# Attention and FFN on one core: five batches' attention packed into FFN tiles 2 to 4, their inputs loaded as fp32, seven-product up-projection in tiles 5 to 8

## The chip, the core and the metric

One core of a Trainium2 chip runs the whole kernel. The metric is the device time of one execution in microseconds (us). The engines are named as in the profile: PE (matrix products; PEld is its weight load), DVE, ACT, POOL, and SP, which here only issues transfers.

## What is computed

```python
# q, k, v: (batch 8, heads 8, sequence 576, head dimension 64), fp32
scores = q @ k.T / sqrt(64)            # masked: a block of 64 rows sees its own and earlier blocks of 64
attn   = softmax(scores) @ v
x      = attn as (8 * 576, 512)
gate   = maximum(x @ w_gate, 0)        # w_gate, w_val: (512, 1536)
out    = (gate * (x @ w_val)) @ w_out  # w_out: (1536, 512), out fp32
```

## The kernel before

**Two halves that share the engines.** The FFN works on 9 tiles of 512 tokens. Tile j below 8 holds the first 512 tokens of batch j; tile 8 holds the last 64 tokens of all eight batches. The attention of a batch is four rounds (one for each pair of heads; round r belongs to batch r // 4). The attention of batch b has to be done before FFN tile b begins.

**A tile of the FFN** (`ffn_gen`). Plain: for each of 12 blocks of hidden units, 4 products for the gate and 4 for the value (L1095, 512 columns each), a relu on ACT (L1105) and a product of both on DVE (L1115). From tile `SEVEN = 2` on, the down-projection (`seven_products`, products in L793) uses a scheme of seven half-size block products in the place of eight, 84 products of 256 columns; it needs sums of hidden values, which DVE makes (L750, 14 calls a tile), copies of PSUM on ACT (L825) and adds on DVE (L829). From tile `UPS = 7` on, the up-projection (`seven_up`, L965) does the same: six units of 28 products of 256 columns. It needs sums of weights, made once on POOL (`up_sums`, L900), copies on ACT, adds on DVE (L992), and products on DVE and POOL (L997, L1001).

**A round of attention.** `visit` (L454) makes the scores of two heads and three groups of exponentials on ACT (L459, L466); `corners` sets the masked blocks to zero on DVE (L1263) or POOL (L1266); `head_av` multiplies by the values (L589, L603) and normalises (DVE, L526 to L535); the result `xnat` is transposed into `xT`, for batches 2 to 7 by a DMA transpose from SP (L638). From batch `FIRST = 3` on, the 64 tail tokens are done inside the rounds; their result goes by `xtail` into `xTt` (L575). `last_keys` (L476) makes the scores of the tail with itself.

**How q, k and v arrive.** Batches 0 to 2 (class `Early`): SP loads fp32 into `stage` tiles (10 of them, which the FFN's sums use too), a compute engine casts to bf16, and then either PE transposes, or (batch 2) SP issues a DMA transpose of 1024 columns into `perm` (L245) and a compute engine reorders `perm` into `qTm` or `kTm` (`unpermute`, L256). Batches 3 to 7 (`load_qkv`, L341): POOL issues loads that cast on their way, 17 to a batch, and SP issues two DMA transposes of 2048 columns (`dma_transposes`, L350) straight into `qTm` and `kTm`, and two for the tails (L119, L120).

**What sets the order.** The order is written out by hand: every piece of work has a name and a place in a table `AT`, and the places count steps of the FFN (one step is one product of 512 columns or two of 256; a tile is 144 or 138 steps). A loop takes the pieces in order of their places, and lets the FFN run up to the place before each. So on each engine the order is fixed, and an engine that waits holds up all that stands behind it in its own queue; between the engines only semaphores count. Names: `s`, `e`, `c`, `a`, `b`, `x` with a round's number are its scores, its last exponential, its corners, the two heads' products with the values, and its transpose into `xT`; `L3` is `last_keys(3)`. In the steady part a round came every 28 steps, and the attention of batch b + 1 lay in tile b:

```python
STEADY = {"s": 2, "e": 8, "c": 15, "a": 22, "b": 26, "x": 26.1}
...
for b in range(4, B):
    base = 144 * (b - 1)
    for i in range(4):
        ...
            AT[f"{n}{r}"] = base + 28 * i + p + (5 if i == 3 and n in "abx" else 0)
```

**PSUM.** Eight banks: four for scores (`sc`, two tiles of two banks), one named `one`, and three that the FFN and attention share (`ffnp`). When the last scores are done, the four of `sc` become the up-projection's banks (`upa`, `upc`).

## Time and profile before

| What | us |
|---|---|
| three runs: median (lowest to highest) | 358.78 (355.13 to 361.32) |
| the profiled execution: its time | 356.78 |
| its span, first to last instruction | 355.0 |
| busy: PE | 340.3 |
| busy: DVE | 214.9 |
| busy: ACT | 196.8 |
| busy: POOL (its loads among it) | 166.2 |

| Part of the span (chain of waits) | from, us | to, us |
|---|---|---|
| tile 2 (batch 3's attention and batch 2's tail in it) | 104.5 | 145.4 |
| tile 3 (batch 4's attention in it) | 145.4 | 182.8 |
| tile 7 (no attention) | 296.1 | 324.2 |

The profiled execution's time is that of the run; the span is what the trace covers, and 1.78 us lie around it. Busy times of engines overlap. Matrix products are pipelined: the mean of one (379 ns for 512 columns) is longer than the distance between two.

### The profile page before, as it was taken

What the parts mean: (1) busy time and instruction counts of PE and PEld (TensorE: products, weight loads), DVE (VectorE), ACT (ScalarE), POOL (GpSimd) and SP (SyncE); (2) the same over time, 40 slices, a digit from 0 to 9 for tenths busy, and PEclk for the clock granted to TensorE, in tenths of its full rate; (3) what the DMA queues carried; (4) which work ended last, traced back from release to release, by engine and by line L of the source; (5) the groups of instructions that cost most, each with busy time, mean ns of one, the idle gap of its engine ahead of it and who ended that gap; (6) DMA issues with size and microseconds to landing.
All of it is one profiled execution on the core that took longest, in us unless ns stands there. A gap on an engine that the chain in (4) does not pass through costs nothing.

```text
span 355.0 us, 8402 instructions
## 1 busy us (share of the span) xinstructions
PE 340.3 (96%) x3277; PEld 216.7 (61%) x3317; DVE 214.9 (61%) x552; ACT 196.8 (55%) x319; POOL 166.2 (47%) x199
## 2 busy tenths in 40 slices
PE   7899999999989999999999999999999999999994
PEld 3544455545434458555765577556855598888883
DVE  4664445668526766367626663567447757787783
ACT  4932756687235573655556554665276626735731
POOL 4647546589905900292009407970291042620630
PEclk9999999999999999999999999999999999999999
DMA  8999989999997997499539973999521013003005
GB/s 245 295 354 373 329 218 274 205 144 160 196 196 82 143 124 157 119 139 130 114 115 137 132 147 111 107 130 154 113 66 24 18 24 118 2 3 118 2 3 118
DMA packets 155496, 50.04 MB, mean 141 GB/s; under 512 B 134464, under 2 KB 151872, under 8 KB 155456
## 3 DMA queue, kind: packets, MB, share of 16 engines
q0 software_dynamic: 70480, 8.85, 47.4%
q1 hardware_dynamic: 79040, 33.96, 46.9%
q10 hardware_dynamic: 5936, 6.69, 5.9%
q8 instruction: 26, 0.43, 0.5%
q14 instruction: 14, 0.11, 0.1%
HBM read 37.75 MB, written 9.44 MB: 133 GB/s over the span
## 4 chain that ended last, share of the span: by engine, by line
PE 84%; ACT 5%; DMA 4%; DVE 3%; issue 2%; POOL 0%; DVEq 0%; POOLq 0%
PE ffnp L1095 37%; PE ffnp L793 12%; PE upa L965 6%; PE one L793 5%; PE ffnp L1199 3%; PE sc L454 3%; PE upc L965 3%; DMA xT<-xnat 2%; PE ffnp L589 2%; PE one L454 2%; DMA stage<-in_moe_w_gate_dram 2%; ACT attnT L418 2%; PE one L589 1%; PE ffnp L965 1%; ACT attnT L459 1%
## 5 line engine op out<-in xcount | busy, mean ns | idle before, releaser
L1115 DVE TENSOR_TENSOR hT<-gate_sb,ffnp 128x512 bf16<-128x512 bf16 x82 | 56.1, 684 | 63.9 <-PE ffnp L1095 33.1
L1095 PE MATMUL ffnp<-xT,wv 128*128 128x512 bf16 x309 | 87.3, 379 | 1.6 <-issue 0.6
L1095 PE MATMUL ffnp<-xT,wg 128*128 128x512 bf16 x301 | 84.9, 379 | 3.0 <-DMA xT<-xnat 1.7
L1105 ACT ACTIVATE gate_sb<-ffnp 128x512 bf16<-128x512 f32 x79 | 47.9, 609 | 49.2 <-PE ffnp L1095 49.2
L459 ACT ACTIVATE attnT<-sc 128x1024 bf16<-128x1024 f32 x56 | 57.6, 1043 | 0.0
L1095 PEld LDWEIGHTS <-wv 128*128 128x128 bf16 x336 | 30.3, 98 | 35.2 <-issue 5.2
L1095 PEld LDWEIGHTS <-wg 128*128 128x128 bf16 x336 | 30.6, 98 | 32.9 <-issue 3.6
L341 POOL DMA_DIRECT2D q_bf<-in_q_dram x20 | 17.9, 913 | 51.4 <-DVE hT L1115 37.2
L825 ACT COPY ob<-ffnp 128x512 f32<-128x512 f32 x21 | 12.3, 585 | 46.2 <-PE ffnp L793 44.7
L793 PEld LDWEIGHTS <-stage 128*128 128x128 bf16 x336 | 32.5, 98 | 3.6
L589 PEld LDWEIGHTS <-attnT 128*128 128x128 bf16 x640 | 26.5, 98 | 12.7 <-issue 1.9
L793 PEld LDWEIGHTS <-hT 128*128 128x128 bf16 x252 | 24.2, 98 | 4.5 <-DVE hT L997 0.7
L466 ACT ACTIVATE attnT<-one 128x512 bf16<-128x512 f32 (+1 forms) x28 | 15.0, 536 | 18.0 <-PE ffnp L454 17.8
L341 POOL DMA_DIRECT2D v_bf<-in_v_dram x30 | 24.2, 876 | 0.7 <-PE one L603 0.6
L1199 PE MATMUL ffnp<-wo,hT 128*128 128x512 bf16 x90 | 22.8, 379 | 0.3
L454 PEld LDWEIGHTS <-kTm 64*128 64x128 bf16 x384 | 13.3, 94 | 14.3 <-issue 8.3
L793 PE MATMUL ffnp<-stage 128*128 128x256 bf16 x168 | 21.4, 273 | 0.0
L793 PE MATMUL ffnp<-wo,hT 128*128 128x256 bf16 x168 | 21.3, 273 | 0.1
L750 DVE TENSOR_TENSOR stage<-hT 128x512 bf16<-128x512 bf16 (+1 forms) x45 | 17.6, 394 | 0.5
L454 PE MATMUL sc<-qTm,kTm 64*128 64x512 bf16 (+1 forms) x168 | 17.8, 305 | 0.0
L341 POOL DMA_DIRECT2D k_bf<-in_k_dram x20 | 17.7, 939 | 0.0
L1001 POOL TENSOR_TENSOR hT<-attnT,gate_sb 128x512 bf16<-128x512 f32 x4 | 4.6, 1162 | 25.1 <-ACT gate_sb L1009 25.1
(185 smaller groups left out, 617.8 us busy)
## 6 DMA issues: line engine op xcount, KB each, us to landing
out_dram<-ob ACTq DMA_DIRECT2D x24, 256.0 KB, 2.4
stage<-in_moe_w_val_dram SPq DMA_DIRECT2D x6, 512.0 KB, 8.3
stage<-in_moe_w_gate_dram SPq DMA_DIRECT2D x6, 512.0 KB, 8.7
stage<-in_moe_w_out_dram SPq DMA_DIRECT2D x6, 512.0 KB, 10.6
q_bf<-in_q_dram POOLq DMA_DIRECT2D x20, 128.0 KB, 4.7
k_bf<-in_k_dram POOLq DMA_DIRECT2D x20, 128.0 KB, 5.8
v_bf<-in_v_dram POOLq DMA_DIRECT2D x20, 128.0 KB, 6.3
stage<-in_v_dram SPq DMA_DIRECT2D x19, 128.0 KB, 5.6
```

The source lines that it names most:

```text
L341: ins = nc.gpsimd.dma_start(dst, part_of)
L454: nc.tensor.matmul(o, kTm[b % 2][head_of(hh), c, hp, :], qT, start=True, stop=True)
L459: return lambda: nc.scalar.activation(at[:, :, lo : lo + 512], sc, AF.Exp, scale=scale)
L466: nc.scalar.activation(at[:, hh, 1024 : 1024 + w], third[hh][:, 0:w], AF.Exp, scale=scale)
L589: nc.tensor.matmul(av[:, p, :], at[:, col : col + 128], v_bf[b % 2][:, c, h, :], start=(p == 0), stop=(c == p), skip_group_check=True,)
L750: ins = (eng or nc.vector).tensor_tensor(out=s(i), in0=a, in1=b, op=op)
L793: nc.tensor.matmul(to, sums.of(c)[which]()[:, 128 * p : 128 * p + 128], right, start=first, stop=(c == 5), skip_group_check=True,)
L965: nc.tensor.matmul(to[:, 256 * f : 256 * f + 256], left(which, u // 2)[:, kc, lo : lo + 128], right[which](kc), start=new and (f, kc) == ( ...
L1095: nc.tensor.matmul(to, (wg, wv)[t][f // 4][:, c, 128 * (f % 4) : 128 * (f % 4) + 128], x[:, c], start=(c == 0), stop=(c == 3),)
L1105: nc.scalar.activation(gate_sb, gate, AF.Relu)
L1115: nc.vector.tensor_tensor(out=h, in0=gate_sb, in1=val, op=AX.mult)
L1199: nc.tensor.matmul(op, hT[f][:, 128 * s : 128 * (s + 1)], wo[f // 4][:, f % 4, n0:n1], start=(f == 0), stop=(f == 11),)
```

## The change

Three things, which go together.

1. Batches 3 to 7 are loaded in the manner of batch 2: SP loads fp32 (q and k in halves of four heads, 512 KB each; v in two pairs of chunks; three tails), POOL, and for some pieces ACT, cast into `half` tiles (7 of them), SP issues four DMA transposes of 1024 columns into `perm`, and POOL reorders them (two copies for each pair of heads). POOL issues no loads any more. `load_qkv` and `dma_transposes` go.
2. Their rounds come every 18 steps from place 315 on, so that batches 3 to 7 are done in tiles 2 to 4. Their first head's product with v uses bank `one`, the second's a shared bank. All products go into `xT` by DMA transposes, as before; `xT` has four buffers in the place of three. Some corners (rounds 12, 13, 16, 21, 28, 29, 31) are zeroed by POOL.
3. `UPS` is 5: tiles 5 to 8 use the seven-product up-projection. Its weight sums move (places about 618 to 738, that is tile 4 and the first steps of tile 5), and those of its second and third part use other buffers. In tiles 2 to 4 the down-projection no longer uses bank `one`, which attention has; it does its products in another order with two banks, and product 5 goes into the bank of product 2. Stores of tiles 4 and 5 go from ACT's queue to SP's (that of the tiles from `UPS - 1` on).

Beside these, some 230 places are given one by one, for pieces of batches 0 to 2 too, most of them moved by a few steps.

```diff
-    UPS = 7
+    UPS = 5
+    HALVES = 7
...
-    def new_bf():
-        return [sb.tile([128, 2048], BF, name=n, bufs=2) for n in ("q_bf", "k_bf")]
+    def new_half():
+        return sb.tile([128, 1024], BF, name="half", bufs=HALVES)
...
-    def load_qkv(b, which, behind=None):
...
-    def dma_transposes(b, ts=(0, 1)):
...
-            xTs[b] = sb.tile([128, 4, 512], BF, name="xT", bufs=3)
+            xTs[b] = sb.tile([128, 4, 512], BF, name="xT", bufs=4)
...
+        if j < UPS:
+            yield from whole(a, 1, cs=range(5))
+            yield from whole(d, 2, cs=(0,))
+            yield from whole(a, 1, new=False, cs=(5,))
+            c11 = kept(a)
+            yield from whole(d, 2, new=False, cs=range(1, 6))
+            sums.step(13)
+            sums.step(14)
+            yield from whole(a, 6, new=False)
+            plus(d, c11)
+            c12 = kept(a)
+            c = d
+            yield from whole(c, 5)
...
         def late_up():
             last = units[5]
             yield from fourth(last)
-            sums.make(1, 1, 0, 2)
             hidden_0(last)
             mult(nc.vector, last, 1, last.s, last.g1)
-            for q, i in ((1, 2), (2, 1), (2, 2), (0, 3), (1, 3), (0, 4), (1, 4)):
+            for q, i in (
+                (1, 1), (1, 2), (2, 1), (2, 2), (0, 3), (1, 3), (0, 4), (1, 4)
+            ):
...
-        STEADY = {"s": 2, "e": 8, "c": 15, "a": 22, "b": 26, "x": 26.1}
+        STEADY = {"s": 0, "e": 6, "c": 12, "a": 24, "b": 28, "x": 28.1}
+        START, STEP = 315, 18
...
+            return {
+                f"Q{b}0": (-100, lambda: e.load_qk(0, 4)),
+                f"Q{b}4": (-92, lambda: e.load_qk(4, 4)),
+                f"V{b}0": (-72, lambda: e.load_v_chunks(0)),
+                f"V{b}1": (-64, lambda: e.load_v_chunks(1)),
+                f"T{b}": (-56, lambda: load_tails(e)),
+                f"K{b}0": (-88, lambda: e.cast_qk(0, 4, [by[n] for n in HOW[f"K{b}0"]])),
+                f"K{b}4": (-76, lambda: e.cast_qk(4, 4, [by[n] for n in HOW[f"K{b}4"]])),
+                f"P{b}0": (-87.9, lambda: e.transpose(0)),
+                f"P{b}4": (-71, lambda: e.transpose(1)),
+                **{
+                    f"u{b}{hp}": (p, unpermute(hp))
+                    for hp, p in enumerate((-62, -55, -42, -34))
+                },
+                f"w{b}0": (-50, lambda: e.cast_v_chunks(0, by[HOW[f"w{b}0"][0]])),
+                f"w{b}1": (-46, lambda: e.cast_v_chunks(1, by[HOW[f"w{b}1"][0]])),
+                f"tc{b}": (-38, lambda: e.cast_tails(True, 0, pool)),
+                f"td{b}": (-26, lambda: e.cast_tails(False, 1, dve)),
+                f"t{b}": (-25, e.transpose_tails),
+                f"L{b}": (9, lambda: last_keys(b)),
+            }
...
+                "K30": ("pool", "act"),
+                "K34": ("act", "pool"),
+                "K50": ("act", "pool"),
+                "K54": ("act", "pool"),
+                "c12": "pool",
+                "c13": "pool",
...
+            base = START + 4 * STEP * (b - FIRST)
...
-                AT[f"U{i}{s}"] = 144 * (4 + min(i, 1)) + 128 + 4 * i + s
-        AT["U23"], AT["U24"] = 144 * 6 + 115, 144 * 6 + 116
+                AT[f"U{i}{s}"] = place_at((288 + 330, 288 + 276 + 118, 288 + 414 + 18)[i]) + s / 8
...
+                "Q40": 295.64,
+                "Q44": 303.64,
+                "K40": 307.64,
+                "P40": 307.74,
...
+                "u40": 329.0,
+                "c12": 329.47,
```

Letters in the new table: `Q` loads q and k of four heads, `V` two chunks of v, `T` the tails; `K`, `w`, `tc`, `td` cast them; `P` transposes `half` into `perm`, `u` reorders `perm`, `t` transposes the tails. The first digit is the batch; the numbers are places in steps, those of the first list relative to the batch's first scores.

More of the change, by code (lines that the diff above doesn't have):

```diff
@@ L886, in up_sums @@
                 four = [sb.tile([128, 1024], BF, name="perm", bufs=4) for _ in range(4)]
-            else:
-                two = new_bf()
-                four = [t[:, 1024 * n : 1024 * n + 1024] for t in two for n in range(2)]
+            elif i == 1:
+                four = [new_half() for _ in range(4)]
+            else:
+                four = [
+                    t[0].rearrange("p c h n -> p (c h n)")[:, 1024 * n : 1024 * n + 1024]
+                    for t in (qTm, kTm)
+                    for n in range(2)
+                ]
             wsums.append([t.rearrange("p (c n) -> p c n", c=2) for t in four])
@@ L1735, with place_at, quarter, unpermute @@
             acts.update(tail_at(b))
-        for b in range(4, B):
-            base = 144 * (b - 1)
+        def place_at(p):
+            if p < 288:
+                return p
+            j, o = divmod(p - 288, 138)
+            return 144 * (j + 2) + min(o, 96) + max(0, o - 96) * 48 / 42
+        def quarter(b):
+            e = Early(b)
+            def unpermute(hp):
+                return lambda: e.unpermute(hp, [by[n] for n in HOW[f"u{b}{hp}"]])
+            return {
[19 more added lines that the diff above has]
+            }
@@ L1738 @@
+        for b in range(FIRST, B):
+            base = START + 4 * STEP * (b - FIRST)
             for i in range(4):
                 r = 4 * b + i
-                here = ("sc", "sc") if i == 3 else ("one", "ffn")
-                acts.update(round_at(r, ("dve", *here, None)))
+                acts.update(round_at(r, (HOW[f"c{r}"], "one", "ffn", None)))
                 for n, p in STEADY.items():
-                    AT[f"{n}{r}"] = base + 28 * i + p + (5 if i == 3 and n in "abx" else 0)
-            acts[f"L{b}"] = lambda b=b: last_keys(b)
```

422 lines of the change are left out of this document (294 added, 128 removed), and 3 rows, old and new, of the table WHEN.

## The prediction

> **What bounds the kernel now.** I read the page's first two parts, then the stretches of single tiles, the chain of waits for the pace inside a tile, PE's waits for what the pace leaves, and last the queues that the change loads.
>
> ```profile
> PE 340.3 (96%) x3277; PEld 216.7 (61%) x3317; DVE 214.9 (61%) x552; ACT 196.8 (55%) x319; POOL 166.2 (47%) x199
> PE   7899999999989999999999999999999999999994
> PEclk9999999999999999999999999999999999999999
> ```
>
> PE is busy in 340.3 of 355.0 us, at full clock in every slice. What is lost lies in the first slices, in one slice near 104 us, and in the last (the stores). No other engine is above 61%. The stretches (columns: length, then busy us of PE, PEld, DVE, ACT, POOL) of an attention tile and of a tile without attention:
>
> ```profile
> 146.00:183.00 37.00, 36.63 (x363) 23.07 (x367) 21.62 (x61) 20.42 (x34) 13.72 (x17) 1.00 1.39 124
> 296.00:324.00 28.00, 27.93 (x254) 24.48 (x252) 21.53 (x41) 15.76 (x29) 10.22 (x9) 1.00 0.11 38
> ```
>
> The first is FFN tile 3 with batch 4's attention inside it: PE idles 0.37 us in 37. The second is tile 7, which has the seven-product up-projection and no attention: 0.07 us idle. So a tile costs what PE's instructions cost, and I price the change by PE's pace. In the chain of waits (start, length, what):
>
> ```profile
> 153.42 4.42 PE ffnp L1095 x20
> 180.27 1.31 PE ffnp L793 x12
> 302.30 0.94 PE upa L965 x8
> ...
> 308.52 0.94 PE upa L965 x8
> ```
>
> The first line is 20 plain products of 512 columns; the last one's own 379 ns (page, group L1095) overlaps nothing, so the pace is (4.42 - 0.38) / 19 = 0.213 us. The second: 12 products of 256 columns at 0.109 us. The third and the fourth mark the same place of the seven-product up-projection, two units apart: 6.22 us, 3.11 a unit. PE's largest wait in mid-kernel, the transposes that the change multiplies, and a load (SP's timeline and the DMA list of 50 to 80 us):
>
> ```profile
> PE ffnp L1095 <- DMA xT<-xnat: 1.7, 2, 1.4
> 57.94 2.71 SPq L245 DMA_TRANSPOSE perm<-q_bf  x1
> 60.75 2.49 SPq L245 DMA_TRANSPOSE perm<-k_bf  x1
> 71.82 2.04 SPq L245 DMA_TRANSPOSE perm<-q_bf  x1
> 73.95 1.28 SPq L245 DMA_TRANSPOSE perm<-k_bf  x1
> stage<-in_q_dram SPq DMA_DIRECT2D x2, 512.0 KB, 5.4
> stage<-in_k_dram SPq DMA_DIRECT2D x2, 512.0 KB, 6.3
> ```
>
> A transpose of 1024 columns holds SP's queue for 1.28 to 2.71 us, mean 2.13; a 512 KB load lands 5.4 to 6.3 us after its issue.
>
> **The change, part by part.** The sum is made against the profiled execution: 356.78 us, of which 355.0 is span and 1.78 lies around it. The median of the three runs, 358.78, is 2.0 above it; I do not add that to the forecast.
>
> *Up-projection of tiles 5 and 6.* Plain: 96 products x 0.213 = 20.4 us. Seven-product: 6 x 3.11 = 18.7 us. Gain 1.7 a tile, 3.5 for two, all of it on PE, which sets the end. If its 168 half-width matmuls ran at half of 0.213, it would be 17.9 and the gain 5.0; I take 3.5, since tile 7 shows the pace with its real weight loads. What comes with it: ACT and DVE work per tile as in the tile 7 line (15.8 and 21.5 of 28 us), which did not hold PE there. The twelve weight sums on POOL (2.12 us each, 25.4) are only moved; the last eight now run around the end of tile 4 and into tile 5, and push POOL's six products per tile (1.16 us each) back by up to 8.5 us. POOL then has about 10 us for 10 us of work before the down-projection needs it: 0 taken, 1 us if it is late.
>
> *Attention of five batches in three tiles instead of five.* PE issues the same instructions: 0. A tile's FFN part is 20.4 + 84 x 0.109 = 29.6 us, so a batch costs 37.4 - 29.6 - 0.4 = 7.4 us of PE, and a round now comes every 18 steps instead of 28: a batch every 72/138 x 29.6 + 7.4 = 22.8 us. In these 22.8 us: ACT has 4 x (2 x 1.04 + 2 x 0.60) + 0.41 = 13.5 of exponentials, 6.3 relus x 0.61 = 3.8, 2.1 copies x 0.585 = 1.2: 18.5, 81%. The stretches 50 to 60 and 70 to 80 us had ACT at 8.3 and 8.6 of 10 with PE at 9.87 and 9.89, so 81% alone costs nothing that shows. DVE: 8 x (0.19 + 0.42 + 0.21) + 1.3 for corners + 6.3 x 0.68 + 7.3 sums x 0.42 + 1.6 x 0.69 = 16.3, 72%.
>
> *Loads and casts.* Out: per batch 12 POOL loads of 0.90 to 0.94 us and five small ones of about 0.7 us, 14.5 us of POOL, and the two 2048-column transposes. In, per batch on POOL: 4 casts x 1.04, 8 reorderings x 1.075, 2 value casts x 1.04, tails 0.61 + 0.39 + 0.40, corners 0.6: 16.9 of 22.8 us. In on SP: 4 transposes x 2.13, 2 tail transposes x 1.2, 4 of xT x 1.22, one of xTt 1.17, 11 loads x 0.55: 23.0 of 22.8 us by the mean, 19.6 if each transpose costs the least row, 1.28. SP is therefore the queue to watch, though its loads are issued about 100 steps (30 us) ahead of use.
>
> *New waits.* No row of before shows these stages in this rhythm. A cast stands 12 to 17 steps behind its load (batch 4: places 295.6 and 307.6; batch 5: 354.4 and 371.0), 3.8 to 5.3 us at 22.8/72 = 0.317 us a step, against 5.4 to 6.3 us to land. So the casting engine stands up to 2.5 us. On POOL, corner zeroing for rounds 12, 13, 16, 21 is queued behind these casts and behind reorderings that wait for a transpose, and PE's products wait for the zeros. On ACT (one cast each of K50 and K54) the relus and exponentials of tile 3 are queued behind, and PE has only three FFN banks to run on with. The stores of tiles 2 and 3 on ACT wait in turn for DMA semaphores shared with SP's late transposes. From below: 0, if the idle stays at 0.37 us a tile. A gain is excluded, since these waits do not exist before. From above: eight casts (two of each of batches 4 to 7) x 2.5 us, half of it reaching PE: +10. Scores have about 59 steps of slack behind the first reordering and most POOL work waits unseen; I take two or three visible stalls of about 1 us: +2.5, nearer the lower end because the rows of a full ACT show none.
>
> *The start of tile 2.* PE stood 1.7 us for xT, whose transposes were queued around 4.6 and 6.4 us ones of batch 3. In the changed order all four perm transposes of batch 3 stand ahead of the first xT of batch 2 by a whole group of loads, and only two tail transposes are between. I take the 1.7 off. From below 0 (SP late for another reason); from above 2.9, the whole idle time of the stretches of 10 us from 100 to 130 (1.77 + 0.69 + 0.41).
>
> *Order inside the down-projection of tiles 2 to 4.* The bank of product 5 is now that of product 2, so PE waits for DVE's add (0.69, behind two sums of 0.42: 1.5 us) under product 6, 12 x 0.109 = 1.3 us: 0.2 a tile at most, 0 taken. The last stores keep their queue and length: 0.
>
> Sum: 356.8 - 3.5 - 1.7 + 2.5 = 354.1 us.
>
> **A rule against the change.** Row first: DVE's copies L256 took 0.97 and 1.01 us at 72.3 us, while POOL was casting, and 0.60 at 77.9, while POOL only issued loads. The Trainium skill, "SBUF — State Buffer", section "Who interferes with whom", says that a VectorE instruction with two SBUF inputs contends with a GpSimd instruction that reads SBUF, and that the later one fully blocks. The copies agree with such a lock; no row shows it for the two-input sums. What the mechanism would do here is the third rival.
>
> **The rivals.**
> 1. *The waits stay hidden.* For it: 0.37 us idle a tile, the 59 steps of slack, and transfers that no longer share the DMA engines with POOL's queue, which took 47.4% of their span. Against it: casts stand nearer to their loads than these take to land. Time with the upper gains: 356.8 - 5.0 - 2.9 = 348.9.
> 2. *SP's queue becomes the bound (slower).* 23.0 us of issue a batch against 22.8 leaves no room for its own waits: each pair of transposes waits in order for its casts (1.04 each, after a landing), and xT, tails and the next loads are behind it. Two such waits of about 2 us make 27.0 a batch, 4.2 over, 21 in five batches. The least spare on the way is at the tails: 36 steps, 11.4 us, less 2.4 of issue and 3.9 to land, 5.1. PE would stand 21 - 5.1 = 15.9: 356.8 - 5.2 + 15.9 = 367.5. It decides from transposes above about 2.1 us each together with waits on SP. Against it: at 1.28 us a transpose SP has 3.2 us to spare a batch, and without POOL's transfers they may be that short.
> 3. *DVE stands behind POOL's copies.* Tiles 2 to 4 have some 42 two-input sums, beside a POOL that reads SBUF 70% of the time, 1.08 us at a stretch: 0.7 x 0.54 = 0.38 us each, 16 us of DVE in about 130, which has 28% free. PE meets it only where products follow two sums directly: 3 x 2 x 0.38 = 2.3: 356.4.
>
> That the change does not do what it says is excluded: the changed program holds 192 plain products fewer and 336 half-width ones more.
>
> **How the numbers follow.** Forecast 0.48, rival 1 0.28, rival 2 0.16, rival 3 0.08. About 2% is what a measurement of this kernel can tell from no change: against the median of 358.78 that is 351.6 to 366.0. Faster by over 2%: rival 1, 0.28. Slower: 0.16. Within: 0.56. Range: from 348, just under rival 1's 348.9, to 365, the forecast with the whole upper end of the new waits (351.6 + 10 = 361.6) and a part of rival 2; some 0.07 is left below and 0.13 above. The likeliest case's own range is 351.6 to 361.6.
>
> **What would show it.** The up-projection: tiles 5 and 6 of 28 us each, like tile 7 now. The rhythm: PE's idle time in tiles 2 to 4 (about 103 to 235 us), under 1.5 us if hidden, 2 to 4 as forecast, over 10 for rival 2. The waits: casts on ACT and POOL idle "until DMA stage", PE waiting for POOL's corner zeros or for relus. The start of tile 2: no PE wait for xT. SP: perm transposes of 1.3 or 2.1 us and more. Rival 3: the 512-column sums above 0.42 us. The prediction is wrong if tiles 5 and 6 take more than 29 us, or if PE stands for SP.

## The result and the profile after

The change makes the kernel slower: 388.0 us (median of four runs, 384.1 to 400.3) against 357.3, a ratio of 1.080 (95% interval 1.065 to 1.095). Two of the four executions were slow ones, the profiled one (400.3 us, granted clock 0.84) among them, so the ratio is that of the other two (384.1 and 385.8), and the lines below are of a second set of runs of the same kernel, unaltered: 388.9 us (388.4 to 389.1) against 356.6, ratio 1.093 (1.089 to 1.097). Later runs are compared with these 388.9. Since the same kernel also took 384.1 us, a version that differs from 388.9 by less than some 5 us is not told from it.

The page of the kernel after (busy time, then the 40 slices):

```profile
PE 345.9 (89%) x3461; PEld 230.2 (59%) x3461; DVE 252.7 (65%) x572; ACT 216.5 (56%) x350; POOL 198.5 (51%) x224
PE   6897999984999999978889599967899999999994
PEclk9999999996999999999899899999999999999999
```

PE idles 387.1 - 345.9 = 41.2 us. The profile of the kernel before that stands ahead of the prediction lacks 40 of PE's 3317 products, so its 355.0 - 340.3 = 14.7 us of idle time are too many. A second profile of that kernel (span 354.4 us, taken with the run again below) has them all:

```profile
PE 343.5 (97%) x3317; PEld 217.0 (61%) x3317; DVE 215.5 (61%) x552; ACT 197.3 (56%) x319; POOL 166.8 (47%) x199
```

By it PE idled 10.9 us, so 30.3 of the 32.7 us that the span grew are idle time. The other 2.4 are PE busy for longer, although it has 3.4 us less to do: it works at a lower clock after some of its waits (the tenth slice of the line PEclk shows 6). Where the time lies, each part counted from the same products of its tile:

| Part of the span, us | before | after |
|---|---|---|
| start to tile 2 | 104.5 | 115.3 |
| tiles 2 to 6 | 191.6 | 212.0 |
| tile 7 | 28.1 | 28.2 |
| tile 8 and the last stores | 30.8 | 31.5 |

The stretches of tiles 2, 3 and 4, which now hold five batches of attention (the third reaches 4 us into tile 5), and of tile 7 (length, then busy us of PE, PEld, DVE, ACT, POOL, the granted clock, the DMA share):

```profile
114.00:161.00 47.00, 44.64 (x519) 27.23 (x518) 34.05 (x92) 30.97 (x48) 26.29 (x31) 1.00 1.06 227
161.00:212.00 51.00, 44.46 (x506) 27.12 (x505) 31.06 (x87) 31.14 (x47) 31.25 (x35) 0.97 1.06 213
212.00:269.00 57.00, 46.98 (x517) 29.33 (x516) 40.61 (x86) 29.12 (x45) 30.48 (x25) 0.97 0.36 83
298.00:326.00 28.00, 27.95 (x253) 24.20 (x251) 21.79 (x40) 15.63 (x29) 10.22 (x9) 1.00 0.11 36
```

PE idles 2.4, 6.5 and 10.0 us in the first three, and no other engine is busy for more than 73% of them. So this is no engine that ran out of room: PE waits in single places. PE's waits (us in total, how many, the longest):

```profile
PE one L397 <- DVE xnat L471: 7.1, 1, 7.1
PE ffnp L1057 <- ACT gate_sb L1067: 4.2, 1, 4.2
PE ffnp L736 <- DVE ob L772: 4.0, 2, 3.2
PE one L397 <- DMA qTt<-q_bt: 2.5, 2, 1.4
PE ffnp L532 <- POOL attnT L1228: 2.4, 1, 2.4
PE ffnp L1057 <- POOL wv L329: 2.2, 1, 2.2
PE upa L926 <- DVE stage L892: 2.0, 2, 1.2
PE ffnp L397 <- DVE hT L1077: 1.8, 3, 0.8
PE upa L926 <- DVE xnat L953: 1.7, 1, 1.7
...
PE ffnp L1057 <- DMA xT<-xnat: 0.5, 1, 0.5
```

DVE, ACT, POOL and DMA release them in turn. The releaser is only the last link; I followed each back to the head of the queue that stood.

*85 to 93 us, 7.1.* SP's timeline, then DVE's, then PE's:

```profile
79.00 6.62 SPq L240 DMA_TRANSPOSE perm<-half  x4
```

```profile
88.29 0.84 DVE L251 COPY qTm<-perm 128x512 bf16<-128x512 bf16 x1 [5.81 <-DMA perm<-half]
...
92.20 0.42 DVE L471 TENSOR_TENSOR xnat<-one,recip 128x256 bf16<-128x256 f32 x1
```

```profile
92.68 0.39 PE L397 MATMUL one<-qTm,kTm 64*128 64x256 bf16 x1 [7.07 <-DVE xnat L471]
```

Of the four transposes of 79.0 us the first two are batch 3's; batch 2's second pair is behind them. DVE has batch 2's reordering at the head of its queue and stands 5.8 us for it, with the normalisation that PE needs behind. The stretch right after it:

```profile
92.00:96.00 4.00, 3.32 (x14) 1.20 (x15) 1.40 (x7) 2.52 (x4) 3.62 (x4) 0.50 0.60 94
```

The granted clock is 0.50 for these 4 us (four products of 512 columns took 1.89 us there and 1.03 a little later). The Trainium skill, "TensorE: Matmul & The Clock Gate", Part 1, says that the array falls to half rate after an idle window of about 3.4 us and comes back after a busy one; the trace agrees for this wait. On the length it does not: after a wait of only 2.4 us, which ended at 185.3 us, the clock was 0.50 from 186 to 188 us, and after one of 3.2 us, which ended at 258.3 us, it stayed at 1.00.

*215 to 219 us, 4.2.* ACT's timeline:

```profile
218.30 0.38 ACTq L610 DMA_DIRECT2D out_dram<-ob  x1
218.78 0.60 ACT L1067 ACTIVATE gate_sb<-ffnp 128x512 bf16<-128x512 f32 x1 [4.65 <-DMA stage<-in_v_dram]
```

A relu does not read v. ACT stood at the store ahead of it, whose data was ready by 214.1 us. By the semaphore that the profile names, the store waited for a load of v that SP had issued late (at 212.3 us, landed 5.3 us later); store and load share no data, so I read it as a semaphore that both use.

*253 to 273 us, 6.9 in four waits.* POOL's weight sums, and DVE's two-input sums beside them:

```profile
255.10 2.30 POOL L861 TENSOR_TENSOR half<-wv,wg 128x1024 bf16<-128x1024 bf16 x1
...
266.45 2.18 POOL L861 TENSOR_TENSOR qTm<-qTm,wv 128x1024 bf16<-128x1024 bf16 x1
```

```profile
255.34 2.33 DVE L693 TENSOR_TENSOR stage<-hT,stage 128x512 bf16<-128x512 bf16 x1
...
263.98 0.41 DVE L892 TENSOR_TENSOR stage<-xT 128x512 bf16<-128x512 bf16 x1
...
266.58 2.34 DVE L892 TENSOR_TENSOR stage<-xT 128x512 bf16<-128x512 bf16 x1
```

The same sum takes 0.41 us alone and 2.34 beside a weight sum: each waits for the whole of one (the last two lines end at 268.63 us on POOL and at 268.92 on DVE). I call this the lock. The Trainium skill, "SBUF — State Buffer", section "Who interferes with whom", states this lock for a VectorE instruction with two SBUF inputs beside a GpSimd instruction that reads SBUF; the trace now shows it for the sums, which that of before did not.

What the change was to bring came in tiles 6 and 7. Two units of the up-projection in tile 6 (chain of waits):

```profile
302.25 0.90 PE upa L926 x8
308.48 0.90 PE upa L926 x8
```

6.23 us for two units, as in tile 7 before, and tiles 6 and 7 take 28.2 us each. Tile 5 takes 32.3 (265.1 to 297.4 us), since waits for the sums beside POOL's weight sums stand at its start. The wait for `xT` at the start of tile 2 is down to 0.5 us; but in the second profile of the kernel before it was only 0.2.

### The profile page after: what moved, and what is told of

Its sections match the earlier page's. It is cut to its first block, busy times and chain, and to the rows that moved or that the text cites. A ratio compares the mean times of both kernels' runs of the same rounds, so it can differ in the third digit from the quotient of the medians.

```text
span 398.5 us, 8866 instructions
## 1 busy us (share of the span) xinstructions
PE 381.6 (96%) x3461; PEld 245.3 (62%) x3461; DVE 248.7 (62%) x572; ACT 217.0 (54%) x350; POOL 198.0 (50%) x224
## 5 line engine op out<-in xcount | busy, mean ns | idle before, releaser
L1057 PE MATMUL ffnp<-xT,wg 128*128 128x512 bf16 x220 | 68.9, 424 | 2.4 <-ACT gate_sb L1067 2.1
L1057 PE MATMUL ffnp<-xT,wv 128*128 128x512 bf16 x232 | 71.2, 422 | 0.0
L1077 DVE TENSOR_TENSOR hT<-gate_sb,ffnp 128x512 bf16<-128x512 bf16 x58 | 39.8, 686 | 43.8 <-PE ffnp L1057 32.6
L1067 ACT ACTIVATE gate_sb<-ffnp 128x512 bf16<-128x512 f32 x55 | 32.8, 601 | 46.1 <-PE ffnp L1057 40.7
L193 POOL CAST half<-stage 128x1024 bf16<-128x1024 f32 (+1 forms) x31 | 27.8, 906 | 44.7 <-DMA stage<-in_q_dram 31.1
L962 POOL TENSOR_TENSOR hT<-attnT,xnat 128x512 bf16<-128x512 f32 x20 | 23.2, 1159 | 10.3 <-ACT xnat L1021 9.9
L953 DVE TENSOR_TENSOR attnT<-ffnp,attnT 128x512 f32<-128x512 f32 x24 | 16.6, 690 | 17.1 <-PE ffnp L926 15.7
L226 POOL CAST v_bf<-stage 128x1024 bf16<-128x1024 f32 x12 | 12.8, 1064 | 26.6 <-DMA stage<-in_v_dram 19.2
L251 POOL COPY qTm<-perm 128x512 bf16<-128x512 bf16 x21 | 22.7, 1080 | 1.8 <-DMA perm<-half 1.3
L953 DVE TENSOR_TENSOR attnT<-upc,attnT 128x512 f32<-128x512 f32 x24 | 16.5, 686 | 10.0 <-PE upc L926 7.2
```

Source lines behind the costliest of these rows:

```text
L193: engs[t](self.half(t, h0 // 4)[:, :, lo : lo + 64 * n].rearrange("p j (h d) -> p h j d", d=64), self.st[t, h0].rearrange("p (h j d) -> p ...
L251: engs[t]((qTm, kTm)[t][self.b % 2][:, :, hp, :].rearrange("p c (n j) -> p c n j", j=4), self.perm[t, hp // 2][:, :, hp % 2, :].rearrange( ...
L953: nc.vector.tensor_tensor(out=out, in0=acc, in1=o, op=AX.add)
L962: eng.tensor_tensor(out=m.h[th], in0=val, in1=gate, op=AX.mult)
L1057: nc.tensor.matmul(to, (wg, wv)[t][f // 4][:, c, 128 * (f % 4) : 128 * (f % 4) + 128], x[:, c], start=(c == 0), stop=(c == 3),)
L1067: nc.scalar.activation(gate_sb, gate, AF.Relu)
```

## The experiments

**The two kernels again.** Theory and rivals at this point: A, new waits in tiles 2 to 4 and ahead of them; B, the up-projection of tiles 5 and 6, or the clock. No edit:

> The changed kernel once more, unaltered, for a profile at the clock of its faster runs (the first profile was taken at a granted clock of 0.844, the kernel's faster runs had 0.98). Theory A (waits): at that clock the profile shows 20 us or more of PE idle time in tiles 1 to 4 (about 55 to 260 us), behind loads, casts and POOL's zeros, and tiles 5 to 8 of 28 us each. Theory B (clock): PE is busy almost throughout tiles 1 to 4 and the time is lost to a lower clock in tiles 5 to 8, which then take 30 us or more each.

388.9 us, read above: A. The kernel before, unaltered:

> The kernel before, unaltered, on the same chip, for its granted clock and span beside the changed kernel's. Theory A: 357 us at a clock near 1.0, whatever the changed kernel's clock. Theory B: the same. If its clock falls as well on this chip, the clock belongs to the chip and not to the change.

357.5 us (356.2 to 359.0), ratio 1.003 (0.999 to 1.007): the kernel before repeats to within 1%.

**The up-projection.**

```diff
-    UPS = 5
+    UPS = 7
```

> The changed kernel with UPS back at 7: attention still packed into tiles 2 to 4 and loaded as fp32, plain up-projection in tiles 5 and 6. Theory A (waits in tiles 1 to 4): the loss stays, 384 + 3.5 = about 388 us. Theory B (the up-projection in tiles 5 and 6 costs the time, by clock or by its waits): 360 us or less.

388.1 us (383.5 to 391.5), ratio 1.085 (1.074 to 1.097). The loss stays, so it does not come from there. Its plain tile 5 takes 29.9 us: the gain of a seven-product tile that nothing holds up is 1.7 us, as forecast. That the time does not rise by 3.4 has a reason in the same place: without the new up-projection in tile 5, DVE's `x` sums are not beside POOL's weight sums.

**One stall at a time.** Theory: five stalls, each with a cause of its own. Rival: one full resource, so that a stall taken out comes back elsewhere.

```diff
-                "U11": 667.31,
+                "U11": 655.0, "U12": 655.1, "U13": 655.2, "U14": 655.3,
...
-            nc.vector.tensor_tensor(out=as_x(t[i - 1]), in0=a, in1=b, op=AX.subtract)
+            marks.append(
+                nc.vector.tensor_tensor(out=as_x(t[i - 1]), in0=a, in1=b, op=AX.subtract)
+            )
```

> Changed: the four weight sums of U1 on POOL are placed a fifth of a tile earlier, ahead of DVE's sums of their tile, and the first sum of U2 on POOL waits for DVE's last x sum (L892), so that POOL's weight sums no longer run beside DVE's two-input sums. Theory (POOL's 2.1 to 2.3 us sums stretch DVE's 0.41 us sums to 2.2 to 2.3 us, and PE waits 6.9 us for them between 253 and 273 us): DVE's L892 and L693 show about 0.42 us, the PE waits for DVE's stage and ob there go, 381 to 384 us (5 to 7 less than the changed kernel). Rival (the sums are late for another cause, such as the order on DVE, and are slow because of what they read): DVE's sums keep 2.2 us, within 2 us of the changed kernel. Rival (one resource bounds the whole stage of tiles 2 to 4, so a stall taken out comes back at the next place): the sums are short but the time is within 2 us of the changed kernel.

377.3 us (375.4 to 381.0), ratio 1.057 (1.048 to 1.066): 11.6 less than the changed kernel, the largest gain of any edit. DVE's `x` sums:

```profile
257.18 0.42 DVE L893 TENSOR_TENSOR stage<-xT,stage 128x512 bf16<-128x512 bf16 x1
257.52 0.42 DVE L893 TENSOR_TENSOR stage<-xT 128x512 bf16<-128x512 bf16 x1
```

Tile 5 takes 28.2 us here. In the stretch from 250 to 275 us PE is busy for 24.7 us in place of 18.1. But in the one from 225 to 250 us it is busy for 0.9 less, since the moved weight sums now hold other sums of DVE there, one of half the columns among them:

```profile
244.60 2.21 DVE L693 TENSOR_TENSOR stage<-hT 128x256 bf16<-128x256 bf16 x1
```

So some 5.6 us are the lock's. The rest of the 11.6 is not, and the wait for `xnat` at 85 us has most of it: it is 2.3 us here and not 7.1, though nothing there was changed. SP came to its four transposes at 76.0 us in this execution and at 79.0 in that of the changed kernel. In ten profiles, a start at 79.0 goes with a wait of 5.9 to 7.1 us, a start at 76.0 to 77.9 with one of 1.8 to 3.8.

```diff
-                "P30": 185.75,
+                "P30": 192.0,
```

> Changed: one number, P30 from 185.75 to 192.0, so that SP issues batch 3's first two transposes behind batch 2's second two and not ahead of them. Theory (the 7.1 us wait of PE for xnat at 85 to 93 us is DVE's reorder copy of batch 2, which stands at the head of DVE's queue until transposes come that SP issues after two others of 1.7 us each): the wait falls below 4 us, the clock granted at 90 to 100 us stays above 0.67, 380 to 384 us (4 to 8 less than the changed kernel). Rival (all four transposes are late because the loads and casts ahead of them are, whichever goes first): the wait stays at 7 us, within 2 us of the changed kernel. Rival (one resource bounds the stage, SP's queue): the wait only moves to batch 3, whose transposes are now later, within 2 us of the changed kernel.

383.9 us (382.8 to 385.9), ratio 1.075 (1.068 to 1.082): 5.0 less, which is no more than the changed kernel's own two sets of runs differ by. The wait falls from 7.1 to 1.8 us, and the clock from 80 to 100 us is 1.00. SP started at 77.6 us here. Since the wait is nearly as small without this edit where SP starts early (2.3 us above), the edit is not shown to be what shortened it.

```diff
-            (nc.scalar if j < UPS - 1 else nc.sync).dma_start(
+            nc.sync.dma_start(
```

> Changed: all stores of the tiles' output are issued by SP and none by ACT. Theory (the 4.2 us wait of PE for ACT's gate at 215 to 219 us is a relu behind a store on ACT's queue, whose issue waits for a transfer of SP's loads to land): the wait for gate_sb goes, 382 to 386 us (2 to 6 less than the changed kernel). Rival (the store blocks whichever queue issues it): the stores now hold SP back, transposes and V loads are later, PE waits for attnT, qTt or xnat instead, 387 to 395 us.

387.4 us (386.0 to 389.1), ratio 1.083 (1.075 to 1.090): the rival, though the 1.4 us alone decide nothing. The wait for the relu is gone, and one of 3.6 us for `hT` has come: DVE now stands for the tail of k, which SP issued later.

```profile
221.16 0.89 DVE L205 CAST k_bt<-stage 64x256 bf16<-64x256 f32 x1 [3.25 <-DMA stage<-in_k_dram]
```

```diff
-                "c12": "pool",
...
-                "c31": "pool",
```

> Changed: the seven corner zeros of the attention that POOL writes are written by DVE as the others are. Theory (the 2.4 us wait of PE for attnT at 183 to 185 us is a corner zero of 0.56 us on POOL behind a cast that waits for a V load): that wait goes, 384 to 387 us (1 to 4 less than the changed kernel). Rival (DVE's queue is as full as POOL's): the zeros come as late from DVE, and the time is within 1 us of the changed kernel or longer, up to 391 us.

390.8 us (383.6 to 392.2), unclear. In the profiled execution the wait for POOL's zeros is gone; waits for relus (4.5) and for `hT` (2.9 and 2.7) stand in its place.

The four edits together, and the early cast of batch 1 put back:

```diff
-                "q0": 32.07,
```

> Changed: the four edits together (POOL's weight sums earlier and apart from DVE's x sums, batch 3's transposes behind batch 2's on SP, stores on SP, corners on DVE), and the cast of batch 1's first q is put back to its place in the kernel before, behind the weight casts that PE waited 2.2 us for. Measured alone against the changed kernel (388.9): 377.3, 383.9, 387.4, 390.8. Theory (each stall has its own cause, so the gains add): 388.9 - 11.6 - 5.0 - 1.4 + 0 to 2, and up to 2 for the cast: 369 to 373. Rival (full queues in tiles 2 and 3 put a new stall where one is taken out): no better than the first edit alone, 376 to 382.

375.7 us (373.5 to 376.6), ratio 1.051 (1.044 to 1.059). That is 13.2 below the changed kernel and 1.6 below the first edit alone, which is no clear difference; it lies between the ranges of theory and rival. It does not decide between them either: the 11.6 of the first edit hold, by its profile, about 5 us of the early start on SP, which the second edit was after as well, and 5.6 + 5.0 + 1.4 = 12.0 would be gains that add. The weight cast's wait and the two long ones are gone; what is left is a dozen of 0.6 to 3.1 us, and 19 us over the kernel before.

**The parts alone.** So I took the change apart: the load path, the rhythm, the order in the down-projection. First the fp32 loads and casts at the old rhythm, with the new order:

```diff
+        for b in range(FIRST + 1, B):
+            base = 144 * (b - 1)
+            for i in range(4):
+                for n, p in slow.items():
+                    AT[f"{n}{4 * b + i}"] = (
+                        base + 28 * i + p + (5 if i == 3 and n in "abx" else 0)
+                    )
+            for n, (p, f) in quarter(b).items():
+                AT[n] = place_at(288 + 138 * (b - 3) + p)
```

> Changed: batches 4 to 7 have their rounds every 28 steps again, batch b + 1 in tile b, as in the kernel before; batch 3's rounds too; the up-projection of tiles 5 and 6 is plain, and the weight sums come in tile 6. The fp32 loads by SP, the casts, the transposes of 1024 columns and the reorderings stay. Theory (the load path costs only because a batch comes every 23 us: its 17 us of POOL and 20 us of SP a batch fit well into 37): PE's idle time from 130 us on under 4 us, 360 to 368, of which the stall of batch 2's reordering at 85 us, which this does not touch, is 4 to 9. Rival (the load path costs wherever it is, since casts and reorderings stand in the queues of POOL, DVE and ACT): 375 to 388.

390.4 us (389.6 to 391.2), ratio 1.093 (1.086 to 1.101). My theory fell: with 37 us a batch it is as slow as with 23. PE's largest wait:

```profile
PE ffnp L736 <- DVE ob L772: 10.8, 5, 2.7
```

Once in each of tiles 2 to 6 PE stands before product 5, whose bank is that of product 2, until DVE's add is done; ahead of the add DVE has two normalisations and two tail casts. I had priced this at nothing. The kernel before with the new order alone, and with the banks of the rounds that go with it:

```diff
-        c = psum_one.tile([128, 512], FP, name="one")
-        yield from whole(c, 5, cs=range(2))
...
+            c = d
+            yield from whole(c, 5)
...
-                here = ("sc", "sc") if i == 3 else ("one", "ffn")
-                acts.update(round_at(r, ("dve", *here, None)))
+                acts.update(round_at(r, ("dve", "one", "ffn", None)))
```

> Changed: in the kernel before, only the order of the down-projection in tiles 2 to 6 (two banks, product 5 in the bank of product 2) and the banks of the rounds (one and a shared one for all of them). Theory (PE waits for DVE's add before product 5, as the run with the old rhythm showed with 2.1 to 2.7 us a tile): PE waits 1 to 2.5 us in each of five tiles for DVE's add, 361 to 370. Rival (the add was late only because DVE's tail casts were slow beside POOL's reorderings, which the kernel before does not have): no wait over 0.8 us, 356 to 360.

362.0 us (361.1 to 363.8), ratio 1.013 (1.009 to 1.017): the theory, 4.7 us, and this is the wait:

```profile
PE ffnp L793 <- DVE ob L829: 5.4, 5, 1.3
```

The load path without it, with the old order and banks; the corners on POOL, the early cast and P30 are put back too:

```diff
-            c = d
-            yield from whole(c, 5)
...
+            c = psum_one.tile([128, 512], FP, name="one")
+            yield from whole(c, 5, cs=range(2))
...
+                here = ("sc", "sc") if i == 3 else ("ffn" if b == 3 else "one", "ffn")
+                acts.update(round_at(r, (HOW[f"c{r}"], *here, None)))
```

> Changed: the load path alone. The rhythm of the kernel before (batch b + 1's rounds in tile b, every 28 steps), its order and banks in the down-projection and its banks for the rounds, its up-projection; corners on DVE; batch 1's first cast at its old place and batch 3's first transposes behind batch 2's second. What is left of the change: batches 3 to 7 by fp32 loads from SP, casts, transposes of 1024 columns and reorderings, mostly on POOL. The run with the old rhythm but the new order in the down-projection (390.4) had 10.8 us of waits for DVE's add, 2.1 to 2.7 a tile, and 6.2 for a corner on POOL and a weight cast. Theory (the new order in the down-projection is a cost of its own, and the path fits in 37 us a batch): no wait for the add over 1 us, 357 to 367. Rival (casts and reorderings in the queues of POOL and DVE cost PE wherever they are): 372 to 385.

387.3 us (386.9 to 394.0), ratio 1.084 (1.080 to 1.088): the rival. The wait for the add is 2.0 us, and another has come in three tiles:

```profile
PE one L397 <- DMA qTt<-q_bt: 8.1, 3, 2.8
```

The tails' transposes stood behind the last `xT` transpose on SP, where I had left them. So I moved them ahead:

```diff
+            early = {f"T{b}": -63.9, f"tc{b}": -46, f"td{b}": -42, f"t{b}": -41}
...
-                AT[f"U{i}{s}"] = 144 * 6 + (45, 75, 115)[i] + s / 8
+                AT[f"U{i}{s}"] = 144 * 6 + (2, 30, 60)[i] + s / 8
```

> Changed against the run with the load path alone (387.3): the transposes of a batch's tails stand 16 steps earlier, ahead of the xT transpose of the last round before them, and the weight sums come 43 to 55 steps earlier in tile 6. Theory (the path itself fits in 37 us a batch, what cost were the 8.1 us of waits for qTt, 2.9 for x sums and 5.4 us lost around them after 300 us): those waits go, 366 to 375. Rival (casts and reorderings hold the queues, so something else is late next): 380 to 390.

392.4 us (389.7 to 392.8), ratio 1.096 (1.091 to 1.100). The wait for qTt is gone, and PE waits for DVE's corners instead; PE's line, and DVE's at the first of the four:

```profile
PE sc L532 <- DVE attnT L1212: 15.8, 4, 5.2
```

```profile
145.87 0.50 DVE L205 CAST k_bt<-stage 64x256 bf16<-64x256 f32 x1 [3.91 <-DMA stage<-in_k_dram]
```

A tail cast now stands on DVE for its load, ahead of the corners. In both places one queue stood for something else's transfer, 2 to 5 us at a time. So the load path at the old rhythm, with rounds in five tiles and the old up-projection, costs 30 to 35 us, as much as the whole change. Both runs keep most of the changed kernel's places for batches 0 to 2: the first product of tile 2 comes at 107.1 and 108.9 us, against 101.9 in the kernel before, and no run tells what of these 5 to 7 us is theirs.

Now the packing alone: the kernel before, with its casting loads, and the changed kernel's places for the rounds:

```diff
-                here = ("sc", "sc") if i == 3 else ("one", "ffn")
-                acts.update(round_at(r, ("dve", *here, None)))
+                acts.update(round_at(r, ("dve", "one", "ffn", None)))
...
+                "L3": 279.55, "s12": 320.86, "e12": 322.22, "c12": 329.47, "a12": 340.22,
...
+                "l4": 275, "d4": 312.0, "lv4": 329.0, "l5": 334.0, "d5": 384.0, "lv5": 403.43,
```

> Changed: the kernel before, with its casting loads by POOL and its transposes of 2048 columns, but with the changed kernel's places for the rounds of batches 3 to 7 (every 18 steps, in tiles 2 to 4), its order in the down-projection, and its up-projection in tiles 5 to 8; the weight sums come at the start of tile 4, ahead of DVE's sums of that tile; q, k and v of batch b are asked for 125 and 58 steps ahead of its first scores. Theory (packing is cheap, what costs is the path of fp32 loads, casts and reorderings in the queues of POOL, DVE, ACT and SP): 350 to 359, PE's idle time from 100 to 250 us under 5 us. Rival (a batch every 23 us is too much for ACT and DVE, or for the transposes on SP, whatever loads it): PE idles over 10 us in tiles 2 to 4, 364 to 380.

376.2 us (374.5 to 378.3), ratio 1.053 (1.043 to 1.063). In time the rival, but of the 23.0 us that PE idles from 100 to 250 us, 19.7 are two waits:

```profile
PE one L476 <- DMA kTt<-k_bt: 13.7, 1, 13.7
PE ffnp L1120 <- DMA xT<-xnat: 6.0, 1, 6.0
```

Both wait for transposes that SP issued late. (This profile lacks 32 products, so the idle time is somewhat less.) I moved what was waiting, or what was in the way:

```diff
-                "L3": 279.55, "s12": 320.86, "e12": 322.22, "c12": 329.47, "a12": 340.22,
+                "L3": 333, "s12": 320.86, "e12": 322.22, "c12": 329.47, "a12": 340.22,
...
-                "l4": 275, "d4": 312.0, "lv4": 329.0, "l5": 334.0, "d5": 384.0, "lv5": 403.43,
+                "l4": 275, "d4": 312.0, "lv4": 329.0, "l5": 334.0, "d5": 402.51, "lv5": 403.43,
```

> Changed against the run with the packed rounds and the casting loads (376.2): batch 3's tail scores (L3) go back to place 333, behind the transpose of its tails that PE waited 13.7 us for, and batch 5's transposes stand behind the last xT transpose of batch 3 on SP, that PE waited 6.0 us for. Theory (those two waits and the lower clock behind them are all that packing costs with these loads): 376.2 - 13.7 - 6.0 - about 7 for the clock = 347 to 353, faster than the kernel before by 1 to 2.5%. Rival (SP's 2048-column transposes of 2.4 to 6.6 us and transfers that land 7 to 9 us after their issue are too much for a batch every 23 us): other waits of the same kind come in their place, 357 to 372.

375.3 us (374.2 to 377.7), ratio 1.051 (1.046 to 1.056). Both are gone, and two new ones have come, 10.9 and 6.8 us for relus; ACT's line at the second and longer of its two stops:

```profile
168.78 1.08 ACT L1130 ACTIVATE gate_sb<-ffnp 128x512 bf16<-128x512 f32 x2 [12.24 <-DMA kTm<-k_bf]
```

As in the changed kernel, a relu stands behind a store whose semaphore a transfer of SP holds, here a 2048-column transpose. Stores of tiles 1 to 3 by SP:

```diff
-                (nc.sync if i else nc.scalar).dma_start(
+                (nc.sync if i or j else nc.scalar).dma_start(
...
-            (nc.scalar if j < UPS - 1 else nc.sync).dma_start(
+            nc.sync.dma_start(
```

> Changed against the second run with packed rounds and casting loads (375.3): the stores of tiles 1 to 3 are issued by SP and not by ACT. Theory (PE's two waits there, 6.8 and 10.9 us for relus, are ACT standing 9.8 and 12.2 us at a store until a 2048-column transpose lands, whose semaphore the store shares): they go, and 17.7 us and part of the clock behind them with them, 350 to 358. Rival (the stores then hold SP, whose transposes are late already): PE waits for xT, qTm or kTm instead, 362 to 376.

370.2 us (369.7 to 371.3), ratio 1.036 (1.032 to 1.040): 5.1 less, and one wait of 14.0 us in place of two. The store is now behind batch 5's transposes on SP, and ACT's next copy into its buffer waits 15.1 us for it. Two ways out of that, stores by POOL with later loads of batches 6 and 7, and SP's stores with later loads and earlier transposes:

```diff
-            nc.sync.dma_start(
+            (nc.gpsimd if j < UPS - 1 else nc.sync).dma_start(
```

> Changed against the run with packed rounds, casting loads and stores on SP (370.2): the stores of tiles 1 to 3 are issued by POOL, and the q and k loads of batches 6 and 7 come 16 to 23 steps later with their transposes 11 to 18 steps later, so that tile 2's stores on POOL are ahead of batch 6's loads. Theory (the 14.0 us wait of PE behind ACT's copy into ob is the price of a store that stood behind transposes, and nothing else is lost in tiles 2 to 4): that wait and 3 to 5 us of low clock go, 349 to 355, under the kernel before. Rival (the stage has no room, so the wait moves to the loads or to the later transposes): 359 to 372.

```diff
-                "l4": 275, "d4": 312.0, "lv4": 329.0, "l5": 334.0, "d5": 402.51, "lv5": 403.43,
+                "l4": 275, "d4": 312.0, "lv4": 329.0, "l5": 334.0, "d5": 384.0, "lv5": 403.43,
```

> Changed against the same run (370.2): stores stay on SP, the q and k loads of batches 6 and 7 and their transposes come later as in the other run of this call, so that batch 5's transposes do not share the DMA engines with batch 6's loads, and batch 5's transposes stand 16 steps earlier on SP, ahead of batch 3's last xT transposes. Theory (the transposes are 2.4 us and not 5 to 7.5 when no casting loads move beside them, so both the xT transposes and the stores behind them are in time): no wait over 3 us, 350 to 357. Rival (SP's order only exchanges which of the two is late): PE waits 4 to 8 us for xT at the start of tile 3, 360 to 368.

372.6 us (368.4 to 374.9), ratio 1.040 (1.034 to 1.046), and 370.3 (369.0 to 372.3), ratio 1.037 (1.033 to 1.041). No gain either time: 9.6 us for the copy in the one, 12.7 us for `xT` in the other, the wait that its rival named, but longer. One long wait stays. How long transfers take to land (median us; the last packed one, then the kernel before, then the changed kernel, which has the packed rhythm but no casting loads):

```profile
xT<-xnat SPq DMA_TRANSPOSE x20, 8.0
qTm<-q_bf SPq DMA_TRANSPOSE x5, 12.8
kTm<-k_bf SPq DMA_TRANSPOSE x5, 12.6
```

```profile
xT<-xnat SPq DMA_TRANSPOSE x24, 3.7
qTm<-q_bf SPq DMA_TRANSPOSE x5, 10.2
kTm<-k_bf SPq DMA_TRANSPOSE x5, 6.9
```

```profile
xT<-xnat SPq DMA_TRANSPOSE x24, 3.4
```

The first block is the longest of the five packed runs: `xT` takes 6.2 to 8.0 us in them, `qTm` 6.6 to 12.8, `kTm` 7.9 to 12.6. So beside the casting loads of a batch every 23 us the transposes for `xT` land about twice as late, and in the same rhythm without these loads they do not. I read the transfers as what bounds the packed stage, since one long wait for them stays whatever is put first; that is argued and not shown. It is not SP's queue alone: in the run with stores on POOL the copy waited for stores that stood on POOL, between waits of 2.4 and 2.6 us for loads of v.

Last, a looser packing, five rounds a tile, old loads and old order, one more seven-product tile:

```diff
-    UPS = 7
+    UPS = 6
...
+            j, n = divmod(r - 17, 5)
+            return 426 + 138 * j + (0, 24, 48, 72, 96)[n]
```

> Changed: the kernel before with its load path and its order in the down-projection, but with one round more in each of tiles 2 to 5 (five in place of four, every 24 steps), so that tile 6 has none and its up-projection has seven products; loads and transposes at the same distance from the first scores as before; the weight sums in tiles 4 and 5. Theory (up-projection gains 1.7 us a tile when nothing waits): 354 to 357, 0.2 to 1% less than the kernel before. Rival (even one round more a tile brings waits for transposes or stores): 359 to 370.

376.9 us (375.4 to 377.9), ratio 1.055 (1.051 to 1.058). The rival: 6.9 us of waits for `xT` and one of 5.6 for a relu, around the start of tiles 2 and 3, where batch 4's loads and transposes now fall too. No version beats the kernel before. In seven of the runs since I took the change apart the time lay even above the range of the rival, by 0.6 to 6.9 us: the rivals were priced too low as well.

## Why the prediction was wrong

- **The up-projection, -3.5.** Right where nothing holds it up: 29.9 us a plain tile, 28.2 with seven products, 1.7 each. But the step "the twelve weight sums on POOL are only moved: 0 taken, 1 us if it is late" failed. Beside DVE's sums they cost PE 6.9 us of waits, and tile 5 took 32.3 us, over the 29 that I had named as a sign of being wrong; with the weight sums apart it took 28.2. Rival 3 had the mechanism; I gave it POOL's copies (0.38 us a sum, 2.3 in all) and not the weight sums, which hold DVE 2.2 us at a time where products follow the sums directly. Its own price was too high: between 114 and 235 us, where POOL casts and reorders, the 22 sums of 512 columns took 0.58 us by the mean against 0.41, so 0.17 more.
- **The start of tile 2, -1.7.** Not a gain to count on: the 1.7 us became 0.5, but they were 0.2 in the second profile of the kernel before, so part of them was luck of one execution. And tile 2 starts 10.8 us later. Some of the 230 places given one by one concern batches 0 to 2, and I priced none of them: a cast put ahead of weight casts (2.2 us of wait for `wv`), and batch 3's transposes ahead of batch 2's (up to 7.1, though when SP gets there counts as well).
- **New waits, +2.5, bounds 0 and +10.** This is the term that was mis-sized. PE idles 30.3 us more, of which some 10 are ahead of tile 2 and 7 the lock; the rest, some 13, is above my upper end, and comes by other waits than I counted. I looked at a cast behind its own load; what cost was what stood behind such a wait on the same engine and belonged to another batch or to the FFN: a normalisation behind a reordering, a relu behind a store, corners behind a cast of v. I had named the last two, but their price was to lie inside the 2.5.
- **Nothing for the clock.** After waits of 7.1 and 4.2 us PE worked at half rate for some us. PE's busy time is 5.8 us above what its work would be (2.4 more, with 3.4 less to do), part of it this; the mean granted clock was 0.982, against 0.994 in the second profile of the kernel before.
- **The order in the down-projection, 0.** Failed: 1.1 us a tile in the kernel before with the new order and its banks (5.4 in five), 2.2 with tail casts ahead of the add. I had summed the add and two sums and left out the normalisations of the round that falls there.
- **Transposes, 2.13 us by the mean, SP at 23.0 us a batch.** Right in size: on SP's timeline of the second run those of 1024 columns take 2.12 us by the mean. Rival 2 asked PE to stand for SP. In the changed kernel it hardly does (2.5 us for qTt). With the old loads in the packed rhythm it does, and there the time is 370; that this is near the 367.5 of that rival is chance, since the 367.5 were worked out for the other load path.
- **Range and chances.** 388 is 23 us above my upper end. Each end was the sum of waits that I could name in a timeline of before, and no row of before could show the ones that came.

What the runs do not settle: what the load path costs by itself at its best. Its two versions alone (387.3 and 392.4) each had a repeated wait that came from my own placing, and with these waits taken off, and nothing put in their place, they would still be some 20 us above the kernel before (387.3 - 8.1 = 379.2, 392.4 - 15.8 = 376.6); the rest is many small waits, the start and the clock, which no run took apart. Nor is it settled why SP comes to its transposes at 76 us in one execution and at 79 in another, nor whether the gains of the single edits add. In the changed kernel itself, places beyond the four edits were not tried.

## What to carry to other kernels

Price a moved piece by what stands behind it on its queue, not by its own length: list, for every instruction that waits for a transfer (a store's semaphore too), the next one behind it that TensorE needs, and ask by how much the transfer may be late. In this kernel every other engine had a quarter of its time free and the order was fixed by hand, and yet neither packing the work closer nor the new load path at the old pace could use that time: what they took away was the slack that hid the waits. A stall taken out of such a stage often came back as another one (a relu's wait of 4.2 us as one of 3.6 for `hT`; in the packed runs 19.7 us in two waits, then 17.7 in two others, then 14.0 in one). Before moving a POOL instruction that reads SBUF, look what two-input sums of DVE it will run beside.

## What the runs showed of the hardware

- A DVE sum of two SBUF tiles of 128x512 bf16 took 0.41 us alone and 2.23 to 2.34 beside POOL's sums of 2.1 to 2.3; one of 128x256 took 0.29 alone and 2.21 beside them. So it was not slowed in proportion, but held until POOL's instruction ended.
- After a wait of 7.1 us the granted clock was 0.50 for 4 us, after one of 14.0 us likewise (0.50 in the 4 us behind it). After one of 2.4 us it was 0.50 as well, after one of 3.2 us it stayed at 1.00.
- ACT stood at a store 4.7 us until a load of v landed, and 9.8 and 12.2 us until a 2048-column transpose did; the profile names no tie between them but a semaphore.
- Transposes for `xT` landed 6.2 to 8.0 us after their issue (medians) beside the casting loads of a packed stage, 3.7 in the kernel before and 3.4 in the changed one, which has no casting loads; those of 2048 columns held SP's queue for up to 7.5 us.
